# The first q and k of an attention batch, transposed at the end of the batch in front of it

## The chip, the cores and the metric

One core of one Trainium2 chip runs one program. The metric is the device time of one execution in microseconds (us). TensorE (PE) multiplies, VectorE (DVE), ScalarE (ACT) and GpSimd (POOL) work on tiles, and SyncE (SP) issues most DMAs; ACT issues some as well. Each engine goes through its own list of instructions in order, and waits where an operand or a buffer isn't ready.

## The reference

Three stages follow each other. Attention on q, k, v of 4 batches, 8 heads, 576 positions, 64 columns:

```python
q_d = q.reshape(B, H, Sd, factor, D).mean(axis=3)      # factor 4: 144 positions; k_d, v_d alike
out_d = sm_attn(q_d, k_d, v_d)
out_up = np.repeat(out_d, factor, axis=2)
mask = np.abs(pos[:, None] - pos[None, :]) < factor    # local part: 7 neighbours
scores = scale * np.matmul(q, k.transpose(0, 1, 3, 2))
...
return (out_up + out_local).astype(np.float32)
```

Its output is x, 2304 tokens of 512 columns. Then come two layers on x:

```python
h = x @ w_in                      # 512 -> 2048
g = h * (1.0 / (1.0 + np.exp(-1.702 * h)))
x = g @ w_out                     # 2048 -> 512
a = x @ w1
b = x @ w2                        # 512 -> 1024
h = a * b @ w3
return (h @ w_out).astype(np.float32)
```

## The kernel before

**Products.** Each large product is written as three matmuls of split operands (`mm3`, lines 118 to 120): low by high, high by low, high by high. The high half is a copy by ACT (line 114), the low half a subtraction, mostly by DVE (line 115).

**Stages of the program.** First `w34` is computed, the product of w3 and the second w_out (`ps_w34`, shown as `ps_w` in the trace, lines 573 to 587); its results leave through `w34s` tiles. Then the first layer goes over the tokens in blocks of 512, 512, 512, 256 and 512. In a block, `h_step` makes `ps_h` from `x_t` and w_in (4 parts kk of the 512 columns, 12 matmuls a step, 16 steps), gelu gives `g_t`, and `y_step`, two steps later, adds up `ps_y` (`ys` when it leaves). `x_t` of a block comes from `x_d` in memory: `tok_load` reads a tile `xr` on SP's queue (line 596), `tok_split` makes high and low. There are two `xr` tiles, so the read of part kk+2 waits until part kk is split. The second layer follows (`ps_ab`, `ps_o`).

**Attention.** A batch has 4 pairs of heads (HP = 4); pair n = 4b + i. A pair goes through four stages, cut into pieces: T transposes q and k (`t_piece`, line 274) and sums each group of 4 positions to `qd` and `kd`; S makes local scores (`ps_s`, line 333) and pooled scores (`ps_sp`, line 352), their maxima and exponentials `el` and `ep`; P transposes the exponentials (`ps_pt`, line 395, copied to `PT` by ACT); V multiplies with values (`ps_vp`, line 410, and `ps_v`, line 422), adds both to `xo` on DVE (line 426) and writes it to `x_d` on SP's queue (line 430). In T, batches 0 and 1 use PE transposes (`ps_t`, line 284) with ACT copies, and POOL sums (lines 294, 296); batches 2 and 3 use DVE transposes (line 280) and DVE sums (line 292).

**Loads.** `att_load` reads q and k of a pair (`s_q`, `s_k`). For the second pair of batches 1 to 3 it is called in `s_pool` (lines 343 and 344); for others in `p_piece`. A batch 0 or 1 load is issued by ACT, later ones by SP.

**What sets the order.** `att_pieces` (line 527) lists the pieces of a batch; a pump hands one out between matmuls. Batch 0 runs beside `w34`, batch b beside block b - 1, one piece for every second call. The last part kk = 3 of block 0's x needs V of pair 3, and the second block's needs V of pair 7. The pump gives only the program's order: a scheduler with costs and priorities then places each instruction on its engine, so a change in the pieces also moves work that it doesn't name. All transposes, scores and value products of attention share two PSUM tiles (tag "t"); `xo`, `w34s` and `ys` share two SBUF tiles (tag "ys").

Of the kernel before, what the change touches and what calls it, by code (L numbers as in the profile page):

```python
# [20 lines left out]
def fused_kernel(ctx, tc, q, k, v, w_in, w_out1, w1, w2, w3, w_out2, out):  # L21
    nc = tc.nc
    B, H, S, D = q.shape
# [9 lines left out]
    HP = H // 2  # L33
# [195 lines left out]
    def head_ap(src, b, hp, tok, dims):  # L229
        off = ((b * H + 2 * hp) * S + tok) * D  # L230
        return bass.AP(src.tensor, src.offset + off, dims)

    def att_load(n, names="qkv", queue=None):
        b, hp = divmod(n, HP)
        queue = queue or nc.scalar
        for name, src in (("q", q), ("k", k)):
            if name not in names:
                continue
            if b >= PE_T:

                st = att.tile([128, S // 32, 32], F32, tag="s" + name, name="s_" + name)
                for i in range(4):
                    nc.sync.dma_start(out=st[i * 32:(i + 1) * 32], in_=bass.AP(
                        src.tensor, src.offset + (b * H + 2 * hp + i // 2) * S * D + i % 2 * 32,
                        [[D, 32], [32 * D, S // 32], [1, 32]]))
                at["s" + name, n] = st
                continue
            st = att.tile([UC, 2, FAC, 2, D], F32, tag="s" + name, name="s_" + name)
            for c in range(2):
                queue.dma_start(out=st[:, c], in_=head_ap(  # L250
                    src, b, hp, c * UC * FAC, [[FAC * D, UC], [D, FAC], [S * D, 2], [1, D]]))
            at["s" + name, n] = st
        if "v" not in names:
            return
        st = att.tile([UC, 2, 2, FAC * D], F32, tag="sv", name="s_v")
        queue.dma_start(out=st, in_=head_ap(
            v, b, hp, 0, [[FAC * D, UC], [S * D, 2], [UC * FAC * D, 2], [1, FAC * D]]))
        at["sv", n] = st
# [15 lines left out]
    def t_piece(n, name, c):  # L274
        if c == 0:
            at[name, n] = att.tile([128, SD, FAC], F32, tag=name + "T", name=name + "T")
        st, dst = at["s" + name, n], at[name, n]
        if n // HP >= PE_T:
            if c == 0:
                nc.vector.transpose(dst.rearrange("p u r -> p (u r)"), st.rearrange("p a b -> p (a b)"))  # L280
        else:
            ps = pst.tile([128, FAC, UC], F32, tag="t", name="ps_t")
            for r in range(FAC):
                nc.tensor.transpose(ps[:, r], st[:, c, r].rearrange("p h d -> p (h d)"), ident[:UC, :UC])
            nc.scalar.activation(dst[:, c * UC:(c + 1) * UC].rearrange("p u r -> p r u"), ps, AF.Copy)
        if c == 1:
            if name == "q":
                d = qd[:, :SD]
            else:
                d = at["kd", n] = att.tile([128, SD], F32, tag="kd", name="kd")  # L290
            if n // HP in QK_V:
                nc.vector.tensor_reduce(d, dst, op=ALU.add, axis=X)
            else:
                nc.gpsimd.tensor_tensor(d, dst[:, :, 0], dst[:, :, 1], op=ALU.add)
                for r in range(2, FAC):
                    nc.gpsimd.tensor_tensor(d, d, dst[:, :, r], op=ALU.add)

    def v_means(n):
        sv = at.pop(("sv", n))
        nc.gpsimd.tensor_tensor(  # L300
            sv[:, :, :, :2 * D], sv[:, :, :, :2 * D], sv[:, :, :, 2 * D:], op=ALU.add)
        vd = at["vd", n] = att.tile([UC, 2, 2, D], F32, tag="vd", name="vd")
        nc.gpsimd.tensor_tensor(vd, sv[:, :, :, :D], sv[:, :, :, D:2 * D], op=ALU.add)
        if n + 1 < B * HP:
            att_load(n + 1, "v")

    def s_exp(n, i0, i1, src, scale):

        mx, sm = at["mx", n], at["sm", n]
        nb = at["nb", n][:, i0:i1]  # L310
        nc.vector.tensor_scalar(nb, mx[:, i0:i1], -scale, None, op0=ALU.mult)
        for i in range(i0, i1):
            nc.scalar.activation(
                at["el", n][:, i] if i < NQB else at["ep", n][:, i - NQB], src(i), AF.Exp, bias=nb[:, i - i0:i - i0 + 1], scale=scale,
                accum_out=sm[:, i:i + 1])

    def s_tiles(n, own_exp):
        at["ep", n] = att.tile([128, NPB, SD], F32, tag="ep", name="ep")
        for name in ("mx", "sm", "nb")[:3 if own_exp else 2]:
            at[name, n] = att.tile([128, NQB + NPB], F32, tag=name, name=name)  # L320
# [18 lines left out]
            s_exp(n, i0, i1, lambda i: e[:, i], SCALE)  # L339

    def s_pool(n, own_exp):
        if n % HP == 0 and n > 0:
            att_load(n + 1, "qk")
        near = n not in LOCAL
        if not near:
            s_tiles(n, own_exp)
        kd, ep = at["kd", n], at["ep", n]
        ps = pst.tile([128, NPB, SD], F32, tag="t", name="ps_sp")
        for j in range(NPB):
            for h in range(2):  # L350
                p = slice(h * D, (h + 1) * D)
                nc.tensor.matmul(ps[p, j], qd[p, j * PB:j * PB + QB], kd[p], start=True, stop=True)
        mx, sm = at["mx", n][:, NQB:], at["sm", n][:, NQB:]
        nc.vector.tensor_reduce(mx, ps, op=ALU.max, axis=X)
        if own_exp:
            s_exp(n, NQB, NQB + NPB, lambda i: ps[:, i - NQB], PSCALE)
        else:
            nc.vector.tensor_tensor(
                ep, ps, mx.unsqueeze(2).to_broadcast([128, NPB, SD]), op=ALU.subtract)
            if near:  # L360
                el, mxl = at["el", n], at["mx", n][:, :NQB]
                nc.vector.tensor_tensor(
                    el, el, mxl.unsqueeze(2).to_broadcast([128, NQB, KW]), op=ALU.subtract)
            nc.scalar.activation(ep, ep, AF.Exp, scale=PSCALE)
            if near:
                nc.scalar.activation(el, el, AF.Exp, scale=SCALE)
            nc.vector.tensor_reduce(sm, ep, op=ALU.add, axis=X)
            if near:
                nc.vector.tensor_reduce(at["sm", n][:, :NQB], el, op=ALU.add, axis=X)
        r = at["sm", n] if near else sm  # L370
        nc.vector.tensor_scalar_add(r, r, 1e-9)
        nc.vector.reciprocal(r, r)
        if near:
            el = at["el", n]
            (nc.vector if n // HP in NM_V else nc.gpsimd).tensor_tensor(
                el, el, r[:, :NQB].unsqueeze(2).to_broadcast([128, NQB, KW]), op=ALU.mult)
        (nc.vector if n // HP in NM_V else nc.gpsimd).tensor_tensor(
            ep, ep, sm.unsqueeze(2).to_broadcast([128, NPB, SD]), op=ALU.mult)
# [133 lines left out]
    def stage(n, what, own_exp):  # L512
        if what == "T":
            return [lambda name=name, c=c: t_piece(n, name, c) for name in "qk" for c in range(2)]
        if n in LOCAL and what in "SPV":
            if what == "S":
                return [lambda: s_pool(n, False)]
            if what == "P":
                return [lambda: p_piece(n, NPH, NPH + 4), lambda: p_piece(n, NPH + 4, NPT)]
            return [lambda: v_pool(n), lambda: l_out(n, 0, HQ), lambda: l_out(n, HQ, NQB)]  # L520
        if what == "S":
            return [lambda: s_local(n, 0, HQ, own_exp), lambda: s_local(n, HQ, NQB, own_exp), lambda: s_pool(n, own_exp)]
        if what == "P":
            return [lambda i=i: p_piece(n, i, min(i + 4, NPT)) for i in range(0, NPT, 4)]
        return [lambda: v_pool(n), lambda: v_local(n, 0, HQ), lambda: v_local(n, HQ, NQB)]

    def att_pieces(b, own_exp, rest):

        n0, out_ = b * HP, []
        for i in range(HP):  # L530
            if i == 0:
                out_ += stage(n0, "T", own_exp) + [None] * rest
            out_ += stage(n0 + i, "S", own_exp)
            if i > 0:
                out_ += stage(n0 + i - 1, "V", own_exp)
            if i + 1 < HP:
                out_ += stage(n0 + i + 1, "T", own_exp)
            else:
                out_ += [None] * rest
            out_ += stage(n0 + i, "P", own_exp)  # L540
        out_ += [None] + stage(n0 + HP - 1, "V", own_exp)
        return out_

    class Pump:
# [441 lines left out]
```

## Time and profile before

| what | value |
|---|---|
| device time, median of 3 runs | 893.88 us (893.79 to 894.19) |
| device time of the profiled execution | 894.5 us |
| its span, first to last instruction | 892.7 us |
| mean granted TensorE clock, share of full speed | 0.988 |
| PE busy | 846.7 us, 95% of the span |
| PE weight loads busy (beside matmuls) | 711.7 us, 80% |
| DVE busy | 602.2 us, 67% |
| ACT busy | 388.0 us, 43% |
| POOL busy | 146.0 us, 16% |

The profiled execution is one run under the profiler; its span is 1.8 us shorter than its device time. Times within the trace count from the start of the span. The `w34` part ends at about 122 us, block 0 at about 261 us; attention is finished before 600 us. The shares are means over stages with different limits, so a stage has to be read by itself.

### The profile page before, as it was taken

Reading aid. Unit: us, or ns where it says so; the run is one execution under the profiler, and the core shown is the slowest. Engines: PE = TensorE matmul, PEld = TensorE weight load, DVE = VectorE, ACT = ScalarE, POOL = GpSimd, SP = SyncE. Lnnn points to the kernel's source line nnn. Section 1 sums busy time; section 2 is a strip of 40 time slices with the busy share of each in tenths; the row PEclk is TensorE's granted clock in tenths of the full one; section 3 lists DMA queues with packets and bytes.
Section 4 is the critical chain, followed back from the end, with each engine's and each line's share of the span. In section 5 each row is a group of like instructions: output and inputs, shape, how many; then the busy total and the mean of one; then the engine's idle time right before and its main releaser. Section 6 shows DMA issues by size and latency. Waiting matters only on the chain.

```text
span 892.7 us, 13582 instructions
## 1 busy us (share of the span) xinstructions
PE 846.7 (95%) x5132; PEld 711.7 (80%) x5132; DVE 602.2 (67%) x1061; ACT 388.0 (43%) x750; POOL 146.0 (16%) x153
## 2 busy tenths in 40 slices
PE   5689979889999999999999999999999999999998
PEld 4567757666777777777789988889999899989996
DVE  5997597889999999747658784343556455555551
ACT  4667566567756344455336564342112211232111
POOL 7525241233232322301200000000000000000000
PEclk9799999999999999999999999999999999999999
DMA  8866574566665341543247889302556364645521
GB/s 231 271 207 164 154 234 145 155 164 179 152 188 111 78 128 43 162 98 70 64 137 277 322 305 366 130 1 68 226 186 262 107 247 165 250 140 217 196 83 71
DMA packets 140598, 150.76 MB, mean 169 GB/s; under 512 B 86898, under 2 KB 121460, under 8 KB 136436
## 3 DMA queue, kind: packets, MB, share of 16 engines
q1 hardware_dynamic: 119424, 141.21, 49.0%
q10 hardware_dynamic: 21108, 8.69, 4.3%
q8 instruction: 40, 0.66, 0.3%
q14 instruction: 26, 0.21, 0.1%
HBM read 117.75 MB, written 32.11 MB: 168 GB/s over the span
## 4 chain that ended last, share of the span: by engine, by line
PE 57%; DVE 3%; issue 1%; ACT 1%; DMA 0%; DVEq 0%; ACTq 0%
PE ps_ab L120 7%; PE ps_ab L118 7%; PE ps_ab L119 7%; PE ps_y L118 4%; PE ps_y L119 4%; PE ps_y L120 4%; PE ps_h L118 4%; PE ps_h L119 4%; PE ps_h L120 4%; PE ps_o L119 4%; PE ps_o L120 4%; PE ps_o L118 4%; DVE prod L484 1%; PE ps_pt L395 0%; DVE ql L487 0%
## 5 line engine op out<-in xcount | busy, mean ns | idle before, releaser
L118 PE MATMUL ps_h<-x_t,w 128*128 128x512 f32 (+1 forms) x320 | 122.5, 385 | 3.0 <-DVE w L115 2.6
L118 PE MATMUL ps_y<-gh,w 128*128 128x512 f32 (+1 forms) x320 | 122.0, 382 | 0.7 <-ACT gh L114 0.7
L119 PE MATMUL ps_h<-x_t,w 128*128 128x512 f32 (+1 forms) x320 | 119.0, 372 | 0.6 <-DVE x_t L115 0.6
L119 PE MATMUL ps_y<-gl,w 128*128 128x512 f32 (+1 forms) x320 | 118.5, 370 | 1.0 <-DVE gl L115 1.0
L120 PE MATMUL ps_y<-gh,w 128*128 128x512 f32 (+1 forms) x320 | 118.8, 371 | 0.0
L120 PE MATMUL ps_h<-x_t,w 128*128 128x512 f32 (+1 forms) x320 | 118.6, 371 | 0.0
L120 PE MATMUL ps_ab<-b_t,a_in 128*128 128x384 f32 x336 | 112.5, 335 | 0.0
L118 PE MATMUL ps_ab<-b_t,a_in 128*128 128x384 f32 x336 | 112.5, 335 | 0.0
L119 PE MATMUL ps_ab<-b_t,a_in 128*128 128x384 f32 x336 | 112.4, 334 | 0.0
L115 DVE TENSOR_TENSOR gl<-g_t,gh 128x512 fp32r<-128x512 f32 (+1 forms) x80 | 56.3, 706 | 55.6 <-ACT gh L114 55.1
L624 ACT ACTIVATE g_t<-ps_h 128x512 f32<-128x512 f32 (+1 forms) x80 | 44.1, 552 | 103.7 <-PE ps_h L120 102.6
L118 PEld LDWEIGHTS ps_h<-x_t,w 128*128 128x128 f32 x320 | 60.3, 189 | 17.1 <-DVE w L115 4.4
L114 ACT ACTIVATE abh<-ab 128x384 fp32r<-128x384 f32 x24 | 12.6, 526 | 137.5 <-DVE ab L749 137.5
L118 PEld LDWEIGHTS ps_y<-gh,w 128*128 128x128 f32 x320 | 60.3, 189 | 12.5 <-issue 2.2
L119 PEld LDWEIGHTS ps_h<-x_t,w 128*128 128x128 f32 x320 | 60.7, 190 | 10.5 <-DVE x_t L115 1.6
L120 PEld LDWEIGHTS ps_h<-x_t,w 128*128 128x128 f32 x320 | 60.5, 189 | 10.4 <-issue 0.2
L120 PEld LDWEIGHTS ps_y<-gh,w 128*128 128x128 f32 x320 | 60.3, 189 | 10.3
L119 PEld LDWEIGHTS ps_y<-gl,w 128*128 128x128 f32 x320 | 60.4, 189 | 10.1 <-DVE gl L115 1.3
L179 DVE SCALAR_TENSOR_TENSOR dec<-dec,st 128x512 int32<-128x512 int32 x72 | 61.3, 863 | 7.4 <-ACT dec L166 6.6
L118 PEld LDWEIGHTS ps_ab<-b_t,a_in 128*128 128x128 f32 x336 | 63.1, 188 | 0.9
L119 PEld LDWEIGHTS ps_ab<-b_t,a_in 128*128 128x128 f32 x336 | 63.1, 188 | 0.9
L120 PEld LDWEIGHTS ps_ab<-b_t,a_in 128*128 128x128 f32 x336 | 63.1, 188 | 0.0
(149 smaller groups left out, 1645.4 us busy)
## 6 DMA issues: line engine op xcount, KB each, us to landing
a_in<-a_d SPq DMA_DIRECT2D x24, 1792.0 KB
st<-in_moe_w_dram SPq DMA_DIRECT2D x32, 512.0 KB
a_d<-ap SPq DMA_DIRECT2D x8, 1792.0 KB
st<-in_moe_w_out_dram SPq DMA_DIRECT2D x24, 512.0 KB
st<-in_moe_w_in_dram SPq DMA_DIRECT2D x16, 512.0 KB
yr<-y_d SPq DMA_DIRECT2D x12, 384.0 KB
out_dram<-osb SPq DMA_DIRECT2D x17, 256.0 KB
s_v<-in_v_dram ACTq DMA_DIRECT2D x15, 288.0 KB
```

What stands on the lines that cost most here:

```text
L114: nc.scalar.activation(hi, raw, AF.Copy)
L115: lo_eng.tensor_tensor(lo, raw, f32(hi), op=ALU.subtract)
L118: nc.tensor.matmul(ps, ll, rh, start=start, stop=False, skip_group_check=more)
L119: nc.tensor.matmul(ps, lh, rl, start=False, stop=False, skip_group_check=more)
L120: nc.tensor.matmul(ps, lh, rh, start=False, stop=stop, skip_group_check=more)
L179: nc.vector.scalar_tensor_tensor(t, t, 3, st[:, :, 0], op0=ALU.logical_shift_left, op1=ALU.bitwise_or)
L484: (nc.vector if o in DVE_V else nc.gpsimd).tensor_tensor(t, at["vl", n][:, o:o + GT], s[:, o].unsqueeze(2).to_broadcast([128, GT, D]), op= ...
L624: nc.scalar.activation(g[:, :n], ps[:, :n], AF.Gelu_apprx_sigmoid)
```

## The change

`att_pieces` no longer puts T of a batch's first pair at the batch's start (except for batch 0, which has nothing in front of it). T of pair 4(b+1), four pieces, stands at the end of batch b instead, ahead of V of the batch's last pair, in place of one empty piece. The two empty pieces that followed T at the start of batches 1 to 3 go too. Batch 0 has 66 pieces where it had 63, batches 1 and 2 have 58 where they had 61, batch 3 has 39 where it had 45. The loads of q and k of the second pair of batches 1 to 3 move from `s_pool` into `t_piece`: each is issued right after the sums of the first pair's q or k.

```diff
@@ t_piece
                 for r in range(2, FAC):
                     nc.gpsimd.tensor_tensor(d, d, dst[:, :, r], op=ALU.add)
+            if n % HP == 0 and n > 0:
+                att_load(n + 1, name)
@@ s_pool
-        if n % HP == 0 and n > 0:
-            att_load(n + 1, "qk")
@@ att_pieces
-            if i == 0:
+            if i == 0 and b == 0:
                 out_ += stage(n0, "T", own_exp) + [None] * rest
...
             out_ += stage(n0 + i, "P", own_exp)
-        out_ += [None] + stage(n0 + HP - 1, "V", own_exp)
+
+        out_ += stage(n0 + HP, "T", own_exp) if b + 1 < B else [None]
+        out_ += stage(n0 + HP - 1, "V", own_exp)
```

Lines of the kernel after are two higher than before from line 297 to 342 and from line 541 on.

**First place: end of `w34`, start of block 0.** PE before, around V of pair 3 (`ps_vp` and `ps_v`; `ps_w_...` is one of the four sums of `w34`):

```order
L119 MATMUL ps_w_927<-w,w3t 128x512
L410 MATMUL ps_vp<-PT,vd 64x144 x4
L422 MATMUL ps_v<-PT,vw 64x64 x10
L120 MATMUL ps_w_927<-w,w3t 128x512
L422 MATMUL ps_v<-PT,vw 64x64 x8
L118 MATMUL ps_w_945<-w,w3t 128x512
```

Nine matmuls of `w34` and the first twelve of `ps_h` follow here before T and S of pair 4. PE after, at the same V:

```order
L120 MATMUL ps_w_980<-w,w3t 128x512
L410 MATMUL ps_vp<-PT,vd 64x144 x4
L422 MATMUL ps_v<-PT,vw 64x64 x18
L335 MATMUL ps_s<-kT,qT 64x72 x10
L118 MATMUL ps_h<-x_t,w 128x512
```

T of pair 4 now stands some twelve matmuls ahead of this V (`ps_t` from s_q, two matmuls of `w34`, `ps_t` from s_k), all of `w34` is in front of V, and the first scores of pair 4 are right behind it. SP's list before, from V's two writes to `x_d` to the read that waits for them (`w_d` is where `w34s` goes):

```order
L430 DMA x_d<-xo 128x320
L430 DMA x_d<-xo 128x256
L267 DMA vw<-in_v_dram 72x2x64
L271 DMA vw<-in_v_dram 72x4x64 x2
L271 DMA vw<-in_v_dram 72x3x64 x2
L267 DMA vw<-in_v_dram 72x2x64
L587 DMA w_d<-w34s 128x512 x2
L596 DMA xr<-x_d 128x512
```

SP's list after, the same stretch:

```order
L149 DMA st<-in_moe_w_out_dram 128x1024
L267 DMA vw<-in_v_dram 72x2x64
L271 DMA vw<-in_v_dram 72x4x64 x2
L589 DMA w_d<-w34s 128x512
L430 DMA x_d<-xo 128x320
L271 DMA vw<-in_v_dram 72x3x64 x2
L267 DMA vw<-in_v_dram 72x2x64
L142 DMA st<-in_moe_w_in_dram 128x4x256
L589 DMA w_d<-w34s 128x512
L430 DMA x_d<-xo 128x256
L149 DMA st<-in_moe_w_out_dram 128x1024
L598 DMA xr<-x_d 128x512
```

A `w34s` write now stands ahead of each `xo` write, where both `xo` writes stood first. A weight load (`st`) that came after this V's writes is ahead of them; on DVE its two decoding steps (lines 173 and 176) stand right in front of the first `xo`.

**Second place: block 0, P of pair 4.** POOL before, from the sums of pair 4 to those of pair 5:

```order
L296 TENSOR_TENSOR qd<-qd,qT 128x144 x2
L294 TENSOR_TENSOR kd<-kT 128x144
L296 TENSOR_TENSOR kd<-kd,kT 128x144 x2
L375 TENSOR_TENSOR el<-el,sm 128x648
L377 TENSOR_TENSOR ep<-ep,sm 128x432
L294 TENSOR_TENSOR qd<-qT 128x144
```

`el` scaled by its sum (line 375) is what P's transposes `ps_pt` of pair 4 read. POOL after:

```order
L302 TENSOR_TENSOR s_v<-s_v 72x4x128
L294 TENSOR_TENSOR qd<-qT 128x144
L296 TENSOR_TENSOR qd<-qd,qT 128x144 x2
L294 TENSOR_TENSOR kd<-kT 128x144
L296 TENSOR_TENSOR kd<-kd,kT 128x144 x2
L375 TENSOR_TENSOR el<-el,sm 128x648
L377 TENSOR_TENSOR ep<-ep,sm 128x432
```

The five sums shown here are those of pair 5: they stand ahead of pair 4's `el`, where they stood behind it. On PE all 16 transposes of pair 5 now stand in front of the six last matmuls of kk = 3, and pair 4's `ps_pt` right behind these.

**Third place: from block 0 to block 1.** ACT before, from the copy that makes the high half of part kk = 1 (`x_t` of line 114) to the exponential of pair 8's `el` (line 366):

```order
L114 ACTIVATE x_t<-xr 128x512
L642 ACTIVATE ys<-ps_y 128x512 x2
L473 ACT_TABLE_LOAD
L473 ACTIVATE s<-s 128x63
L114 ACTIVATE x_t<-xr 128x512 x2
L642 ACTIVATE ys<-ps_y 128x512 x2
L624 ACT_TABLE_LOAD
L624 ACTIVATE g_t<-ps_h 128x512 x2
L114 ACTIVATE gh<-g_t 128x512 x2
```

Two gelus later the exponential of `el` follows. ACT after, from the copy of part kk = 0:

```order
L114 ACTIVATE x_t<-xr 128x512
L626 ACTIVATE g_t<-ps_h 128x512
L114 ACTIVATE gh<-g_t 128x512
L473 ACT_TABLE_LOAD
L473 ACTIVATE s<-s 128x63
L644 ACTIVATE ys<-ps_y 128x512 x2
L366 ACTIVATE el<-el 128x648
L364 ACTIVATE ep<-ep 128x432
L114 ACTIVATE x_t<-xr 128x512 x2
L644 ACTIVATE ys<-ps_y 128x512 x2
L114 ACTIVATE x_t<-xr 128x512
```

Pair 8's exponentials stand ahead of the copies of parts 1 and 2, where they stood behind all four parts. On PE, after V of pair 7 there are now 36 matmuls of `ps_y` where 24 stood, then part 0 of one step (3 matmuls), `ps_s` of pair 8, part 0 of the next step (3), `ps_sp`, and then part 1; before, parts 0 and 1 of two steps (12 matmuls) stood ahead of `ps_s`.

## Rows read from the trace of the kernel before

**Rows 1.** Windows: busy us of each engine (x instructions), then granted clock, DMA share, GB/s.

```profile
122.00:137.00 15.00, 10.74 (x88) 8.35 (x87) 12.50 (x21) 8.03 (x14) 6.29 (x7) 0.89 0.85 263
255.00:270.00 15.00, 15.00 (x109) 11.65 (x105) 14.39 (x28) 9.31 (x14) 6.48 (x4) 1.00 0.75 200
```

**Rows 2.** Timeline of PE, V(3) to T(5): start, us, operation, [idle before <- releaser].

```profile
118.87 0.69 PE L422 MATMUL ps_v<-PT,vw 72*64 72x64 f32 x16
...
121.65 0.39 PE L118 MATMUL ps_h<-x_t,w 128*128 128x512 f32 x1
...
128.12 1.54 PE L333 MATMUL ps_s<-kT,qT 64*64 64x72 f32 x36
133.18 1.66 PE L352 MATMUL ps_sp<-kd,qd 64*64 64x144 f32 x12 [3.52 <-POOL kd L296]
...
136.21 0.61 PE L120 MATMUL ps_h<-x_t,w 128*128 128x512 f32 x1
...
137.12 0.41 PE L284 MATMUL ps_t<-ident,s_q 72*128 72x72 f32 x4
```

**Rows 3.** Timeline of POOL, the sums of pair 4.

```profile
130.38 0.89 POOL L294 TENSOR_TENSOR kd<-kT 128x144 f32<-128x144 f32 x1
131.35 1.77 POOL L296 TENSOR_TENSOR kd<-kd,kT 128x144 f32<-128x144 f32 x2
```

**Rows 4.** Timeline of SP's queue, a weight load and the writes of V(3).

```profile
103.43 0.38 SPq L142 DMA_DIRECT2D st<-in_moe_w_in_dram  x1
...
120.99 0.99 SPq L430 DMA_DIRECT2D x_d<-xo  x2
```

**Rows 5.** Timeline of DVE, that weight load's first decoding step, and xo of V(3).

```profile
107.55 0.43 DVE L173 TENSOR_SCALAR st<-st 128x512 int32<-128x512 int32 x1 [0.54 <-DMA st<-in_moe_w_in_dram]
...
120.49 0.48 DVE L426 TENSOR_TENSOR xo<-ps_v,od 128x320 f32<-128x320 f32 x1
```

**Rows 6.** Timeline of ACT, the wait for the write of xo, and T(4)'s copies.

```profile
124.32 1.09 ACT L586 ACTIVATE w34s<-ps_w 128x512 f32<-128x512 f32 x2 [3.07 <-DMA x_d<-xo]
...
127.37 1.39 ACT L285 ACTIVATE kT<-ps_t 128x288 f32<-128x288 f32 x2
```

**Rows 7.** Timeline of PE in block 0, where it waits in P(4).

```profile
157.36 0.63 PE L395 MATMUL ps_pt<-ident,el 128*72 128x128 f32 x4 [1.74 <-ACT kT L285]
...
161.42 0.30 PE L395 MATMUL ps_pt<-ident,el 128*72 128x128 f32 x1 [1.32 <-ACT PT L396]
```

**Rows 8.** Timeline of PE from V(7) to the first product of block 1.

```profile
254.03 1.27 PE L422 MATMUL ps_v<-PT,vw 72*64 72x64 f32 x36
...
260.84 0.39 PE L118 MATMUL ps_h<-x_t,w 128*128 128x512 f32 x1
```

**Rows 9.** Timelines of SP's queue and ACT: the read of block 1's last parts.

```profile
259.93 0.82 SPq L596 DMA_DIRECT2D xr<-x_d  x2
...
262.88 1.28 ACT L114 ACTIVATE x_t<-xr 128x512 fp32r<-128x512 f32 x2 [1.04 <-DMA xr<-x_d]
```

**Rows 10.** Groups by line: operation, count | busy us, mean ns | idle before, releasers.

```profile
L354 DVE TENSOR_REDUCE mx<-ps_sp 128x3 f32<-128x432 f32 x16 | 9.6, 599 | 9.7 <-PE ps_sp L352 9.7
L362 DVE TENSOR_TENSOR el<-el,mx 128x648 f32<-128x648 f32 x8 | 6.8, 847 | 0.0
L366 ACT ACTIVATE el<-el 128x648 f32<-128x648 f32 x8 | 5.9, 742 | 1.3 <-DVE el L362 1.2
L364 ACT ACTIVATE ep<-ep 128x432 f32<-128x432 f32 x12 | 6.7, 561 | 4.8 <-DVE ep L358 4.1 <-POOL vd L303 0.7
L280 DVE STREAM_TRANSPOSE qT<-s_q 128x576 f32<-128x576 f32 x8 | 6.1, 768 | 0.0
L367 DVE TENSOR_REDUCE sm<-ep 128x3 f32<-128x432 f32 x12 | 7.1, 594 | 2.2 <-ACT ep L364 2.2
L115 DVE TENSOR_TENSOR x_t<-xr,x_t 128x512 fp32r<-128x512 f32 (+1 forms) x20 | 13.4, 682 | 6.6 <-ACT x_t L114 6.5
L375 POOL TENSOR_TENSOR el<-el,sm 128x648 f32<-128x648 f32 x12 | 16.2, 1352 | 61.7 <-DVE sm L372 54.6 <-ACT g_t L624 4.3 <-ACT dec L166 2.9
```

## The prediction, made before the changed kernel ran

> **What bounds the kernel now.** I read the windows first. In the stretch from block 0 to block 1 PE is busy for all of its 15 us, at a granted clock of 1.00 [rows 1]; at the end of `w34` and the start of block 0 it is busy for 10.74 of 15 us, at 0.89 [rows 1]. So PE is the bound nearly everywhere, what moves to other engines is worth nothing by itself, and a change of order pays or costs only by the waits of PE that it takes away or puts in. The timeline of PE then shows the one large wait in the second stretch: after the scores of pair 4 PE stands for 3.52 us, until POOL has finished `kd` [rows 2]. POOL's rows say why: `kd` takes 0.89 and 1.77 us and starts only at 130.38 [rows 3], after the sums of q, which need T(4). T(4) itself stood late on PE. That wait is what the change is about. Behind it `ps_sp` takes 1.66 us and the products of part kk = 3 take 0.61 us where they take 0.39 us before it [rows 2]: TensorE runs at the lower of its two levels there (1.2 in place of 2.4 GHz). A mean of 0.89 over 15 us is 3.3 us at the half level, so at most 1.65 us more are lost. The old stall is worth 3.5 + 1.65 = 5.2 us. Two more waits stand in P(4), 1.74 us for ACT's copy of kT and 1.32 us for a copy to PT, 3.1 us together [rows 7]. From V(7) into block 1 there is none.
>
> **The change, part by part.** The number of products, transposes, sums and loads of q and k stays the same; they move. The work of T on PE is 16 transposes a pair, four in 0.41 us [rows 2], so 1.6 us, in the order before as after. The loads that move to `t_piece` are issued earlier or at the same place, and nothing on PE waits for them in the trace before: nothing is put down for them, and if that cover were gone it would be a wait of PE in T(5), which is inside the bounds below. Two empty pieces less at the start of a batch cost PE nothing. What counts is order, at three places.
>
> *First place, V(3) to kk = 3.* T(4) ahead of V(3) puts `kd` out of the way: the wait of 3.52 us for it goes. What is late next? V(3) itself. Before, its last products ended at 118.87 + 0.69 = 119.56, with 2.1 us of `w34` and the first products of block 0 behind it [rows 2]. Now all of `w34`, which ends at 121.65 [rows 2], and T(4), 1.6 us, stand ahead: V(3) ends near 123.3. On DVE the decoding of a weight load stands ahead of the first `xo`; such a load took 4.1 us from issue to use (103.43 to 107.55) [rows 4, 5]. How late it comes here the trace can't show; between 0 and 3 us, taken as 1.5, so the first `xo` starts near 124.9 and ends at 125.4. Its write to memory: issue at 120.99, and ACT, which waited for it, goes on at 124.32 [rows 4, 6], so 3.3 us. The second `xo` has no tile of its own until that write has landed, since a `w34s` tile now lies between the two: 125.5 + 3.3 = 128.8. With 0.5 us on DVE [rows 5] and a second write of 3.3 us it has landed at 132.6. The read of `xr` follows on SP: 2.95 us from issue to ACT's copy (259.93 to 262.88) [rows 9], 135.6. High half 0.6, low half 0.7 [rows 9, 10], then the last four products, 1.0 to 1.7 us: 138.3. Before, the same work (kk = 3, and all of T(5), which now stands ahead of it) would be over at 137.12 + 1.6 = 138.7 [rows 2]. So the old stall of 5.2 us is gone and a chain of two writes and a read, one behind the other, eats it up: -0.4 us, between -5.2 (all of the chain covered) and +2.
>
> How long a write takes decides this, so I weigh a rule on it. The rows show 3.3 us for a write and 2.95 us for a read. The Trainium skill (DMA: Bandwidth & Descriptors, Anatomy of one DMA — SWDGE (gpsimd) path) gives a DMA about 2.0 us plus its bytes at 436 GB/s, for the gpsimd path, where these are SP's. By that an estimate for 164 KB, 131 KB and 262 KB in a row is 7.3 us where the rows give 9.6, and the sum would end 2.3 us lower, at 897.8. The rows are SP's own DMAs, so I keep them.
>
> *Second place, P(4).* PE's next work behind kk = 3 is the transposes of pair 4's `el`. Before, POOL scaled `el` ahead of pair 5's sums; now these stand in front. They need T(5)'s copies of kT, and ACT makes those behind the high half of kk = 3 (136.2): the exponential of ep 0.56, kT 0.7, the exponential of el 0.74, kT 0.7 [rows 6, 10] is 138.9. Then `kd` 0.89 + 1.77 [rows 3] and `el` 1.35 [rows 10]: 142.9. PE stands from 138.3: +4.6 us. Queued behind that wait are all products of block 0's third step; who waits for them is ACT with its gelus. This gap hangs on kk = 3 with the same distance whenever that comes, so its lower end is 2 (some of POOL's sums done earlier), its upper 6. In return T(5) is long finished when P(4) runs on, and the old 3.1 us in P(4) should go; I take 2.5 of them, between 0 and 3.1.
>
> *Third place, block 0 to block 1.* Count from the end of V(7), t. Before, 24 products fill the time from 255.3 to 260.84 [rows 8], 0.23 us each; part 0 and part 1 follow, then scores. Now: 36 products 8.3, part 0 of a step 0.7, `ps_s` 1.54 [rows 2], part 0 of the next step 0.7, `ps_sp` about 1.0 (1.66 at the lower clock) [rows 2], together t + 12.2. Then PE needs the high half of part 1, which ACT makes behind pair 8's exponentials, and those need the scores just made: DVE's maximum 0.60, its subtraction 0.85, exponentials 0.74 and 0.56, copy 0.6 [rows 9, 10]: t + 15.5. PE waits 3.3 us. Two products of the high half follow (t + 16.0); the low half stands on DVE behind the subtraction of ep, a transpose of 0.77 for T(8), two sums of 0.6 to 0.85 [rows 10], and needs 0.7 itself: about t + 17.1, 1.1 us more. Sum +4.4 us where before has no wait. Bounds: 3.3 if the low half is in time, 5.9 if the read of the last part (its tile is free only after part 1 is split) and the scaling of `el` on POOL add their 1.5. The read of part 1 itself isn't late: before, a read queued behind V(7)'s writes was in use 7.6 us after V(7) ended (255.3 to 262.88) [rows 8, 9].
>
> *Elsewhere* (pair 12, blocks 1 and 2) parts 0 to 3 of the next block are split ahead of the exponentials, as before: 0, plus or minus 1.5.
>
> **The sum**: -0.4 + 4.6 - 2.5 + 4.4 = +6.1 us. Against the profiled execution of 894.5 us (span 892.7) that is 900.6; the median of the runs is 0.6 lower, so 900.0 us.
>
> **The rivals.**
> *It goes the other way, faster.* One mechanism: the chain behind V(3) is covered. If the weight load is early and POOL has the sums of pair 5 done before `el` is asked for, the old stall goes whole (-5.2), the tangle in P(4) goes too (-2.5), and the third place costs its 3.3: -4.4, 889.5 us. It decides at kk = 3: its high half would have to be on ACT before 132, four us sooner than reckoned. For it: `kd` is the largest wait of this part [rows 2], and the DMAs run at 0.85 of their share there [rows 1], so a quieter queue may be faster. Against it: the order puts V(3) 3.7 us later whatever the DMAs do.
> *It comes out even.* The first place gains 2 us more than the -0.4, the wait in P(4) is 2 in place of 4.6, the rest as reckoned: -2.4 + 2 - 2.5 + 4.4 = +1.5, 895.4, within 0.2%.
> *It is worse: the clock falls too.* The row is the old stall: 3.52 us of waiting, then products at 1.2 GHz, 1.65 us lost. The new waits of 4.6 and 3.3 us are as long; with the same loss behind each the time is 900.0 + 3.3 = 903.3. The Trainium skill (TensorE: Matmul & The Clock Gate, HAM oscillation — how this bites in real kernels) has this as a rule: a wait for data long enough makes the engine start again at the lower clock. The trace agrees after 3.52 us [rows 2].
> *It doesn't do what it says*: the transposes do stand ahead of V(3) and V(7) in the order of PE, so no chance is given to it.
>
> **How the numbers follow.** Forecast 0.52, with its own range 896 to 903; clock as well, 0.16; even, 0.17; faster, 0.15. A measurement of this kernel tells about 0.2% (1.8 us) from no change, so faster means under 892.1, slower over 895.7: 0.15, 0.17, 0.68. The predicted time is that of the likeliest case, 900.0. For the range, the upper end takes the worse case with 1.7 of the third place's and the second's upper bounds, 905; the lower end leaves out the faster case: 892.
>
> **What would show it.** In the profile after: no wait of `ps_sp` for `kd` near 130; instead a wait of `ps_s` or `ps_h` for `xo` and for the last `x_t`, two writes of `xo` over 3 us apart; a wait of `ps_pt` for `el` of line 375, 4 to 5 us, near 140; waits of `ps_h` for ACT's and DVE's `x_t` near 270, 3.3 and 1.1 us, in a stretch that had none; P(4) without its two waits. I am wrong if `x_t` of block 1 is there when PE comes to it, or if PE has other work between V(3) and kk = 3 than the list says; then the time falls under 896.

## The result: slower, and by twice what was reckoned

The changed kernel takes 906.11 us (median of 4 runs, 902.95 to 909.59); the kernel before took 893.84 in the same comparison. The ratio is 1.0145, with a 95% interval of 1.0106 to 1.0184. The direction is as forecast, the size is not: 12 us for a forecast of 6, and above the range of 892 to 905. The profiled execution took 904.0 us, 9.5 more than the one of before; times below are read from it.

PE's busy time rose from 846.7 to 851.1 us with the same 5132 instructions, and the mean granted clock fell from 0.988 to 0.975. From the page of the kernel after (engine: busy us, share of the span, instructions):

```profile
span 901.9 us, 13590 instructions
...
PE 851.1 (94%) x5132; PEld 715.5 (79%) x5132; DVE 605.7 (67%) x1061; ACT 381.3 (42%) x746; POOL 148.8 (16%) x153
```

**Where the time went.** Equal work has to be compared, so I cut both traces at the first product of a block. Block 1 starts at 260.84 before and at 260.86 after: all that happened at the end of `w34` and in block 0 comes to nothing. Block 2 starts at 379.32 and at 390.75. Block 1 alone, windows of before and of after (columns as in [rows 1]):

```profile
260.84:379.32 118.48, 117.43 (x813) 90.17 (x812) 106.21 (x174) 56.76 (x86) 36.11 (x27) 1.00 0.46 113
```

```profile
260.86:390.75 129.89, 120.88 (x813) 92.35 (x812) 104.20 (x170) 52.15 (x84) 35.95 (x26) 0.96 0.41 101
```

Both hold 813 matmuls. Block 1 is 11.4 us longer: PE is idle 9.0 us (129.89 - 120.88) in place of 1.05 (118.48 - 117.43), and busy 3.45 us longer for the same work, at a granted clock of 0.96 in place of 1.00. What follows block 1 is 2.2 us shorter (511.1 for 513.4 us to the end of the span); that goes with pair 12's move, as shown below. So the whole loss is in block 1, and about two thirds of it at its start; the rest stands between 345 and 361, where PE waits twice and the lower clock level comes back (before, the waits there are 0.50 and 0.55 us). PE after:

```profile
349.44 0.95 PE L352 MATMUL ps_sp<-kd,qd 64*64 64x144 f32 x12 [1.58 <-DVE el L338]
...
355.86 0.80 PE L422 MATMUL ps_v<-PT,vw 72*64 72x64 f32 x20 [1.64 <-issue]
...
357.01 0.63 PE L119 MATMUL ps_h<-x_t,w 128*128 128x512 f32 x1
```

**The start of block 1**, timeline of PE after. In the kernel before, block 1 starts at 260.84 [rows 8] and PE has no listed wait until 345.

```profile
260.86 0.39 PE L118 MATMUL ps_h<-x_t,w 128*128 128x512 f32 x1
...
261.63 1.35 PE L335 MATMUL ps_s<-kT,qT 64*64 64x72 f32 x36
...
266.18 0.95 PE L352 MATMUL ps_sp<-kd,qd 64*64 64x144 f32 x12 [2.31 <-DVE el L338]
270.35 1.22 PE L118 MATMUL ps_h<-x_t,w 128*128 128x512 f32 x2 [3.21 <-ACT x_t L114]
271.62 0.80 PE L119 MATMUL ps_h<-x_t,w 128*128 128x512 f32 x1
...
273.50 0.63 PE L120 MATMUL ps_h<-x_t,w 128*128 128x512 f32 x1
...
275.07 0.39 PE L119 MATMUL ps_h<-x_t,w 128*128 128x512 f32 x1
```

PE waits 2.31 us for DVE (line 338, which reads the scores of `ps_s` that came before; `ps_sp` needs their place in PSUM), then 3.21 us for the copy of part 1. The products behind take 0.63 us in place of 0.39: the lower of the two clock levels, until about 275.

**Why the copy is late.** In the timeline of ACT after, part 1 is copied behind pair 8's exponentials, at 269.68:

```profile
252.64 0.63 ACT L114 ACTIVATE x_t<-xr 128x512 fp32r<-128x512 f32 x1 [4.21 <-POOL vd L305]
...
268.58 0.74 ACT L366 ACTIVATE el<-el 128x648 f32<-128x648 f32 x1 [7.01 <-DVE el L362]
269.23 0.55 ACT L364 ACTIVATE ep<-ep 128x432 f32<-128x432 f32 x1
269.68 1.13 ACT L114 ACTIVATE x_t<-xr 128x512 fp32r<-128x512 f32 x2
```

Before, parts 0 and 1 were copied at 248.49 and 255.05, so that PE had 12 products of two steps in hand. ACT before, then PE at pair 8's first scores:

```profile
248.49 0.62 ACT L114 ACTIVATE x_t<-xr 128x512 fp32r<-128x512 f32 x1
...
255.05 0.63 ACT L114 ACTIVATE x_t<-xr 128x512 fp32r<-128x512 f32 x1 [2.22 <-POOL vd L303]
```

```profile
263.65 0.71 PE L333 MATMUL ps_s<-kT,qT 64*64 64x72 f32 x14
```

The difference starts on SP's queue. Its timeline before, around the end of block 0 (start, us of issuing):

```profile
249.24 0.38 SPq L596 DMA_DIRECT2D xr<-x_d  x1
249.66 0.97 SPq L243 DMA_DIRECT2D s_q<-in_q_dram  x2
255.84 0.34 SPq L430 DMA_DIRECT2D x_d<-xo  x1
```

And after:

```profile
245.53 1.50 SPq L243 DMA_DIRECT2D s_q<-in_q_dram  x3
247.08 2.58 SPq L243 DMA_DIRECT2D s_k<-in_k_dram  x4
254.08 1.34 SPq L430 DMA_DIRECT2D x_d<-xo  x2
...
259.14 0.85 SPq L598 DMA_DIRECT2D xr<-x_d  x2
```

The read of part 1 stood ahead of V(7)'s writes, at 249.24. After, the loads of pair 9's q and k, which the change moved into T of pair 8, stand there (eight DMAs, one of them at 242.54), and part 1 is read behind V(7)'s writes, at 259.14. SP issues nothing from 249.66 to 254.08, so it isn't the time that the loads take on the queue that makes the read late, but its place in SP's list, which is fixed when the program is built. It is in memory in good time all the same: in split_pool, below, a read issued at 260.11 is in use at 262.98, and here ACT idles for 7.01 us before the exponentials; but in ACT's list the copy now stands behind them.

**The first two places.** Timeline of PE after, from V(3) on:

```profile
117.97 1.29 PE L422 MATMUL ps_v<-PT,vw 72*64 72x64 f32 x36
122.35 1.47 PE L335 MATMUL ps_s<-kT,qT 64*64 64x72 f32 x20 [3.09 <-DVE xo L426]
...
126.47 0.63 PE L118 MATMUL ps_h<-x_t,w 128*128 128x512 f32 x1
...
136.43 0.74 PE L284 MATMUL ps_t<-ident,s_k 72*128 72x72 f32 x4 [1.32 <-DVE ep L358]
...
139.22 0.63 PE L120 MATMUL ps_h<-x_t,w 128*128 128x512 f32 x1
143.31 1.07 PE L395 MATMUL ps_pt<-ident,el 128*72 128x128 f32 x4 [3.47 <-POOL el L375]
...
147.60 0.63 PE L120 MATMUL ps_h<-x_t,w 128*128 128x512 f32 x1
...
148.99 0.40 PE L118 MATMUL ps_y<-gh,w 128*128 128x512 f32 x1
```

The first product of `ps_y` starts at 148.99; before it started at 140.37, with twelve of pair 5's transposes and four of pair 4's `ps_pt`, 1.9 us by the lengths before [rows 2], [rows 7], still to come that now stand in front. So block 0 is some 6.7 us late there, and none of it is left at 260.86.

### The profile page after: what moved, and what is told of

The parts are those of the page before. It is cut to its first block, busy times and chain, and to the rows that moved or that the text cites. A ratio compares the mean times of both kernels' runs of the same rounds, so it can differ in the third digit from the quotient of the medians.

```text
span 901.9 us, 13590 instructions
## 1 busy us (share of the span) xinstructions
PE 851.1 (94%) x5132; PEld 715.5 (79%) x5132; DVE 605.7 (67%) x1061; ACT 381.3 (42%) x746; POOL 148.8 (16%) x153
## 4 chain that ended last, share of the span: by engine, by line
PE 61%; DVE 19%; DMA 10%; issue 4%; ACT 3%; SPq 1%; POOL 1%; ACTq 0%; POOLq 0%; DVEq 0%
PE ps_ab L120 6%; PE ps_ab L118 6%; PE ps_ab L119 6%; PE ps_h L118 4%; PE ps_h L119 4%; PE ps_h L120 4%; PE ps_y L118 4%; PE ps_y L119 4%; PE ps_y L120 4%; PE ps_o L120 4%; PE ps_o L119 4%; PE ps_o L118 4%; DVE dec L179 3%; DMA st<-in_moe_w_in_dram 3%; DMA st<-in_moe_w_dram 2%
## 5 line engine op out<-in xcount | busy, mean ns | idle before, releaser
L118 PE MATMUL ps_h<-x_t,w 128*128 128x512 f32 (+1 forms) x320 | 126.4, 397 | 3.9 <-ACT x_t L114 3.7
L119 PE MATMUL ps_h<-x_t,w 128*128 128x512 f32 (+1 forms) x320 | 122.1, 382 | 0.3 <-DVE x_t L115 0.2
L120 PE MATMUL ps_h<-x_t,w 128*128 128x512 f32 (+1 forms) x320 | 121.4, 380 | 0.0
L115 DVE TENSOR_TENSOR gl<-g_t,gh 128x512 fp32r<-128x512 f32 (+1 forms) x80 | 58.5, 734 | 61.5 <-ACT gh L114 60.9
L118 PEld LDWEIGHTS ps_h<-x_t,w 128*128 128x128 f32 x320 | 62.0, 195 | 17.6 <-ACT x_t L114 4.4
L120 PEld LDWEIGHTS ps_h<-x_t,w 128*128 128x128 f32 x320 | 62.3, 195 | 11.1 <-issue 0.2
L119 PEld LDWEIGHTS ps_h<-x_t,w 128*128 128x128 f32 x320 | 62.3, 195 | 10.9 <-DVE x_t L115 2.1
L179 DVE SCALAR_TENSOR_TENSOR dec<-dec,st 128x512 int32<-128x512 int32 x72 | 57.3, 807 | 5.1 <-ACT dec L166 4.6
```

The costliest lines, as they stand in the source:

```text
L115: lo_eng.tensor_tensor(lo, raw, f32(hi), op=ALU.subtract)
L118: nc.tensor.matmul(ps, ll, rh, start=start, stop=False, skip_group_check=more)
L119: nc.tensor.matmul(ps, lh, rl, start=False, stop=False, skip_group_check=more)
L120: nc.tensor.matmul(ps, lh, rh, start=False, stop=stop, skip_group_check=more)
L179: nc.vector.scalar_tensor_tensor(t, t, 3, st[:, :, 0], op0=ALU.logical_shift_left, op1=ALU.bitwise_or)
```

## Experiments

The runs of the kernel before that stood beside these lay between 887 and 902 us, so what is compared are ratios to the runs beside them, with their intervals. "Block 1" is the time from the first product of block 1 to that of block 2 in the profiled execution, as above (118.5 before, 129.9 after). Idle is the sum of PE's listed waits in it.

| kernel | median us | ratio to before, 95% interval | block 1 starts | block 1, us | its idle, clock |
|---|---|---|---|---|---|
| before | 893.84 | 1 | 260.8 | 118.5 | 1.1, 1.00 |
| after | 906.11 | 1.0145 [1.0106, 1.0184] | 260.9 | 129.9 | 8.9, 0.96 |
| loads_only | 892.28 | 0.9995 [0.9971, 1.0020] | 258.7 | 118.4 | 1.0, 1.00 |
| t4_only | 899.42 | 1.0068 [1.0045, 1.0091] | 261.1 | 121.6 | 3.7, 1.00 |
| t4_noload | 899.09 | 1.0073 [1.0043, 1.0103] | 261.2 | 121.8 | 3.6, 1.00 |
| t4_t12 | 898.30 | 1.0049 [1.0023, 1.0074] | 261.7 | 122.9 | 3.6, 0.99 |
| t8_only | 904.21 | 1.0122 [1.0091, 1.0152] | 262.1 | 130.5 | 10.9, 0.96 |
| t8_noload | 891.65 | 0.9969 [0.9942, 0.9996] | 260.9 | 119.3 | 1.6, 1.00 |
| t8t12_noload | 890.77 | 0.9964 [0.9937, 0.9991] | 261.5 | 119.2 | 1.6, 1.00 |
| q8_only | 902.67 | 1.0060 [1.0021, 1.0099] | 255.6 | 128.4 | 7.5, 0.97 |
| after_l9 | 897.05 | 1.0049 [1.0021, 1.0078] | 263.9 | 122.7 | 5.3, 1.00 |
| t4t8_noload | 909.34 | 1.0180 [1.0122, 1.0239] | 264.1 | 129.8 | 6.9, 0.96 |
| t_noload | 903.51 | 1.0097 [1.0063, 1.0130] | 264.1 | 129.6 | 6.9, 0.96 |
| after_xo | 905.94 | 1.0144 [1.0098, 1.0190] | 259.3 | 132.3 | 11.2, 0.95 |
| split_pool | 903.22 | 1.0105 [1.0052, 1.0157] | 261.6 | 128.3 | 6.5, 0.96 |
| pad2 | 904.72 | 1.0121 [1.0057, 1.0184] | 261.2 | 128.7 | 9.3, 0.96 |
| pe_b0 | 897.96 | 1.0045 [1.0020, 1.0070] | 262.4 | 125.5 | 4.8, 0.97 |
| pe_b1 | 901.40 | 1.0089 [1.0060, 1.0118] | 260.4 | 129.2 | 3.4, 1.00 |

### Which part of the change: t4_only, t8_only, loads_only

Theory A put the loss at the start of block 1, with T of pair 8; rival B into block 0, with T of pair 4 and the lower clock.

```diff
@@ t4_only, against after
-            if i == 0 and b == 0:
+            if i == 0 and b != 1:
...
-        out_ += stage(n0 + HP, "T", own_exp) if b + 1 < B else [None]
+        out_ += stage(n0 + HP, "T", own_exp) if b == 0 else [None]
@@ t8_only, against after
-            if i == 0 and b == 0:
+            if i == 0 and b != 2:
...
-        out_ += stage(n0 + HP, "T", own_exp) if b + 1 < B else [None]
+        out_ += stage(n0 + HP, "T", own_exp) if b == 1 else [None]
```

In both, only the moved pair's load moves with it.

> Only T of pair 4 moves to the end of batch 0 (with the load of pair 5's q and k); pairs 8 and 12 as before. Theory A (the loss sits where block 0 turns into block 1, and comes with T of pair 8): within 2 us of before, 892 to 896, and no wait of PE near 260 to 275. Rival B (the loss is the chain behind V of pair 3 and the slow clock behind its waits, never given back): 900 or more.

> Only T of pair 8 moves to the end of batch 1; pairs 4 and 12 as before. Theory A: slower than before by about 8 us, 901 to 904, with ps_sp waiting some 2 us, ps_h waiting some 3 us for ACT's x_t and about ten products at the lower clock behind it. Rival B: within 3 us of before.

> The kernel before, with only the loads of pairs 5, 9 and 13 moved from the scores to the transposes. Both theories: no change that can be measured, 892 to 896. If it is over 898, the loads crowd the DMA queues and carry a part of the loss.

T of pair 8 alone loses 11 us, nearly all of the change's loss, in block 1 (130.5 us). The form differs: PE has pair 8's next transposes in its list ahead of part 1, and waits there for POOL:

```profile
275.38 1.50 PE L397 MATMUL ps_pt<-ident,el 128*72 128x128 f32 x6 [9.38 <-POOL el L377]
```

The loads by themselves cost nothing, as long as T stands where it stood. T of pair 4 fits neither theory: it loses about 6 us by the medians, but in the profiled execution (897.8 us, one of its fastest) nothing before block 1 starts (261.1); block 1 is 3.1 us longer there, and the other 3 us aren't located. So the chain behind V(3) isn't the loss, and T of pair 4 isn't free.

### Does block 0 give back what it loses: after_xo, pe_b0, pe_b1

In after_xo the chain behind V(3) is shortened; its first product of `ps_y` starts at 145.1 in place of 149.0.

```diff
@@ after_xo, against after: v_local
-        xo = g2p.tile([128, NB], F32, tag="ys", name="xo")[:, :(i1 - i0) * QB]
+        xo = g2p.tile([128, NB], F32, tag="g" if n == HP - 1 and i0 else "ys", name="xo")[:, :(i1 - i0) * QB]
@@ pe_b0 (j == 0) and pe_b1 (j == 1), against before: h_step
+            for _ in range(2 if j == 0 and 2 <= f < 8 and kk == 0 else 0):
+                mm3(ps[:, :n], w[:, 0, c], w[:, 1, c], xh[kk][:, :n], xl[kk][:, :n], True, True)
```

> The kernel after, but the second xo of pair 3 takes a tile that lies idle then (that of g_t), so it doesn't wait for the first one's write. Theory A: the last part of block 0's x comes some 3 us sooner, but the time hardly falls, 903 to 907, since block 0 gives that loss back anyway. Rival B: 3 us or more faster than the kernel after, 900 to 903.

> The kernel before with 36 products more in block 0: in six of its steps the products of part 0 are made three times, and only the last time counts. That is 36 x 0.23 = 8.2 us more of PE. If block 0's length is set by DVE, which decodes and splits weights there, most of it vanishes: 893 to 897. If PE sets it: 900 to 903.

> The kernel before with the same 36 extra products (8.2 us of PE), now in block 1: six of its steps make the products of part 0 three times, only the last counts. If block 1 is bound by PE they cost in full: 900 to 903. If it has room as block 0 had: 896 or less.

Of the 3.9 us that after_xo gains early, 1.5 are left when block 1 starts, and the time is that of the kernel after. With 8.2 us more of PE's work in block 0, block 1 starts 1.6 us later than before: block 0 has some 6.6 us of room for PE. DVE is busy there for 46.16 of 48 us in the kernel after, 47.48 before (windows 210 to 258); that DVE sets block 0's length is likely by this, but not shown. The total of pe_b0 is still 0.45% above before: in its profiled execution (902.21 us, the slowest of its runs) block 1, whose start is ordered otherwise again, is 7 us longer. With the same work in block 1 (pe_b1), that block is 10.7 us longer and the time 0.9% (8 us) more. So a us of PE's work cost little in block 0 and all of itself in block 1.

### Is it the queueing behind pair 8's exponentials: split_pool, pad2

```diff
@@ split_pool, against after: tok_split
+        if j == 1 and kk in (1, 2):
+            nc.gpsimd.tensor_copy(xh[kk][:, :n], t[:, :n])
+            nc.gpsimd.tensor_tensor(xl[kk][:, :n], t[:, :n], f32(xh[kk])[:, :n], op=ALU.subtract)
+        else:
+            split(t[:, :n], xh[kk][:, :n], xl[kk][:, :n], nc.vector)
-        split(t[:, :n], xh[kk][:, :n], xl[kk][:, :n], nc.vector)
@@ pad2, against after: att_pieces
+            if i == 0 and b == 2:
+                out_ += [None] * (4 + rest)
```

> The kernel after, but the high and low halves of parts 1 and 2 of block 1's x are made by POOL, whose list has room there, so they no longer stand behind pair 8's exponentials on ACT and its sums on DVE. Theory A (that queueing is the loss at the start of block 1): PE's wait of 3.2 us for ACT's x_t goes, the wait of ps_sp before it stays; 3 to 5 us faster than the kernel after, 900 to 903. Rival C (it only moves to the next wait): same as the kernel after, 904 to 908.

> The kernel after, with six empty pieces at the start of batch 2, as many as T and the two empty ones took before, so that pair 8's scores come as late in the program as before though T is done. On ACT parts 1 and 2 of block 1's x then stand ahead of pair 8's exponentials. Theory A: 5 to 8 us faster than the kernel after, 898 to 901. Rival D (T of pair 8 at the end of batch 1 costs by itself, where V of pair 7 comes later): 903 or more.

Both remove the wait they aim at, and the next one in the list takes its place. In split_pool the wait for `x_t` is gone, and pair 8's transposes wait, with the lower clock ahead of them and behind them; in pad2 the high half is in time, and the low half, on DVE behind pair 8's scores, isn't. PE of split_pool, then of pad2:

```profile
266.54 0.95 PE L352 MATMUL ps_sp<-kd,qd 64*64 64x144 f32 x12 [1.89 <-DVE el L338]
...
270.65 0.63 PE L120 MATMUL ps_h<-x_t,w 128*128 128x512 f32 x1
...
275.46 2.18 PE L395 MATMUL ps_pt<-ident,el 128*72 128x128 f32 x9 [3.43 <-POOL el L375]
```

```profile
267.23 1.04 PE L352 MATMUL ps_sp<-kd,qd 64*64 64x144 f32 x12 [3.18 <-DVE el L338]
...
272.69 0.79 PE L119 MATMUL ps_h<-x_t,w 128*128 128x512 f32 x1 [3.27 <-DVE x_t L115]
```

Theory A had 900 to 903 for split_pool and 898 to 901 for pad2, so it was too narrow: the queueing isn't the whole loss. What both still have in common with the kernel after is that PE comes to pair 8's scores with only part 0 of block 1 in hand.

### Why only part 0: t8_noload, after_l9, q8_only

Theory E: the moved load of pair 9 puts the read of part 1 late. In t8_noload and t_noload the edit is the kernel t8_only or after with `att_load` left in `s_pool`; in after_l9 only pair 9's is put back; q8_only moves only the first two pieces of T of pair 8.

```diff
@@ after_l9, against after
-            if n % HP == 0 and n > 0:
+            if n in (HP, 3 * HP):
                 att_load(n + 1, name)
@@ s_pool
+        if n == 2 * HP:
+            att_load(n + 1, "qk")
```

> Only T of pair 8 moves and no load does. Theory E: 892 to 897, where the same kernel with its load moved took 904. Theory A: 902 or more.

> The kernel after, with only the load of pair 9's q and k back in the scores. Theory E (that load on SP's queue ahead of part 1 is the loss): 5 us or more faster than the kernel after, 895 to 901. Theory F (with T of pair 4 moved too, block 0 ends in another order, and the start of block 1 stalls whatever that load does): 902 to 907.

> Only q's half of T of pair 8 moves, with the load of pair 9's q; k's half and its load stay at the start of batch 2. The read of part 1 stands behind V of pair 7 in this order too, and PE meets pair 8's scores ahead of part 1. Theory E and A alike: slower than before by 3 to 10 us, 896 to 903, less than with all of T.

Without the load, T of pair 8 moves for nothing or a little less than nothing (0.9969), where with it 1.0122 was measured: 1.5% hangs on where eight DMAs stand in SP's list. Part 1 is then read ahead of V(7)'s writes again, and copied ahead of the exponentials. t8_noload, SP, then ACT:

```profile
248.29 0.38 SPq L598 DMA_DIRECT2D xr<-x_d  x1
...
256.23 1.78 SPq L430 DMA_DIRECT2D x_d<-xo  x2
```

```profile
254.50 0.62 ACT L114 ACTIVATE x_t<-xr 128x512 fp32r<-128x512 f32 x1
...
263.06 1.39 ACT L114 ACTIVATE x_t<-xr 128x512 fp32r<-128x512 f32 x2
...
269.17 0.75 ACT L366 ACTIVATE el<-el 128x648 f32<-128x648 f32 x1
```

In the changed kernel itself, putting pair 9's load back (after_l9) makes block 1 7.2 us shorter (129.9 to 122.7), and the ratio falls from 1.0145 to 1.0049. That block starts 3.1 us later, though, so that at its end 4.1 of the 11.4 us are given back. What is left in it, 4.2 us, is as much as T of pairs 4 and 12 costs there without T of pair 8 (t4_t12: 122.9). In q8_only, with a half of T and of the load moved, block 1 is nearly as long as in the kernel after (128.4), but it starts 5.2 us sooner than before, so that its end is 4.7 us late.

Over all kernels, in the six whose SP reads part 1 behind V(7)'s writes (after, after_xo, split_pool, pad2, t8_only, q8_only) block 1 takes 128.3 to 132.3 us. Of the ten others without extra products it takes 118.4 to 122.9 in eight, and 129.6 and 129.8 in t_noload and t4t8_noload. So the late read comes with the loss every time, but the loss comes without it too.

### What pairs 4 and 12 cost: t4_t12, t4_noload, t4t8_noload, t8t12_noload, t_noload

> T of pairs 4 and 12 moves, T of pair 8 stays at the start of batch 2. Theory A: as with pair 4 alone, 896 to 901, so pair 12's move costs nothing. Otherwise 903 or more.

> Only T of pair 4 moves, no load. Theory F: as with its load, 897 to 902, the loss in block 1 (its length over 121 us where before has 118.5), not in block 0. Theory E: 892 to 896.

> The kernel after, but the loads of q and k of pairs 5, 9 and 13 stay in the scores, as before; only the transposes move. Theory E (the moved loads of pair 9 stand on SP's queue ahead of the read of part 1 of block 1's x; without them part 1 is read ahead of V of pair 7, as before, and PE has products of two parts in hand): 893 to 898, no wait over 1 us between 255 and 280. Theory A (pair 8's scores come too early whatever the loads do): 902 or more.

> T of pairs 4 and 8 moves, no load. Theory F: as with pair 12 too, 900 to 906. If 892 to 897, pair 12's move is what costs when no load moves.

> T of pairs 8 and 12 moves, no load; pair 4 as before. Theory F: as with pair 8 alone and no load, 889 to 894. If pair 12's move costs: 896 or more.

Pair 12's move costs nothing: t8t12_noload against t8_noload and t4_t12 against t4_only are the same within their intervals, and t_noload against t4t8_noload is 0.8% faster with it. What follows block 1 takes 509.3 to 512.2 us in the eight kernels that move it (mean 510.6) and 510.3 to 513.5 in the ten that don't (512.7), so it seems to gain some 2 us there. Pair 4's costs about 0.7% with its load or without; what of it the profiled executions show, 3.1 and 3.3 us, is in block 1. Pairs 4 and 8 together without loads lose as much in block 1 as the changed kernel, though part 1 is read early there. Theory E had 893 to 898 for t_noload, which took 903.51, so the load isn't the whole cause; t4t8_noload, at 909.34, lies above theory F's 900 to 906. PE's waits in t4t8_noload are other ones again:

```profile
267.53 0.50 PE L118 MATMUL ps_h<-x_t,w 128*128 128x512 f32 x1 [1.11 <-ACT x_t L114]
...
354.26 0.95 PE L352 MATMUL ps_sp<-kd,qd 64*64 64x144 f32 x12 [3.05 <-DVE el L336]
```

V(7)'s last products end on PE at 254.97 there, but DVE adds the second half of them only at 262.03, behind other products and sums of its own (lines 463 and 465), so the write, and the read of the part that needs it, come late. Theory F, that T of pair 4 makes block 0 end in another order and the start of block 1 stalls, isn't shown: the waits at the start, from 267 to 270, are 2.0 of that kernel's 6.9 us, and the longest stands at 354.26. Which of the moved instructions does it wasn't isolated, and after_l9, with the loads of pairs 5 and 13 moved and pair 9's not, does better than the kernel with none moved (t_noload). Why pair 4's move costs stays open.

t8t12_noload, the change without T of pair 4 and without the loads, is the fastest of all: 0.9964, with an interval that ends at 0.9991, some 3 us under the kernel before. t8_noload (0.9969) can't be told from it.

## Why the prediction went wrong, step by step

- **The loads, put down as nothing: this step failed.** The prediction says that nothing on PE waits for the moved loads, and nothing is put down for them; it looked for who waits for them, not for who stands behind them. Pair 9's eight DMAs stand on SP's queue where the read of part 1 stood, part 1 falls behind V(7)'s writes, and PE comes to pair 8's scores with part 0 alone. The working even had that read behind V(7)'s writes, but asked only whether it would be in memory in time (it was), not what had put it there, and took the third place's waits for an effect of the transposes. Measured: T of pair 8 alone has 1.0122 with that load and 0.9969 without; in the changed kernel, with that one load put back, block 1 is 7.2 us shorter and the ratio falls by 0.0096, some 8.6 us. This isn't a share that adds up with the rest: with all three loads put back (t_noload) block 1 is as long as in the changed kernel, by other waits, whose cause stays open.
- **The third place: right in place and kind, too small.** Reckoned: 3.3 us for the high half and 1.1 for the low half, 4.4 together, 5.9 as the bound. Measured: 3.21 for the high half, as worked out, and none for the low half, since the two products ahead of it took 1.22 us at the lower clock level; but also 2.31 for `ps_sp`, which the sum took as running on. It waits for DVE's `el` of line 338, and DVE had four operations of lines 484 and 487 first, 261.65 to 265.6. Later in block 1 come the two waits of 1.58 and 1.64 us. Idle time in block 1 rose by 8.0 us.
- **The lower clock, made a rival with a chance of 0.16: it came.** It made 3.45 us in block 1 alone, for the same 813 matmuls; 3.3 was the figure for both places. More than half of that is behind the start and the rest behind the wait of 1.64 us at 355.86, where none was looked for. In block 0 it came too (0.63 us a product from 123.75 to 128, from 136.9 to 139.7 and from 144 to 148.5), but block 0 gave that back.
- **The first place: the last part in time by luck, the net wrong way round.** The wait for `kd` went. V(3) ended at 119.26, not 123.3, since the work ahead of it ran sooner (PE busy for all of 90 to 106 at clock 1.00, where before had 15.37 us at 0.89). The writes and the read took 3.5, 4.3 and 4.4 us (122.32 to 125.83, 126.40 to 130.74, 130.74 to 135.16), 12.3 in all, more than the 3.3, 3.3 and 2.95 of the rows. By the Trainium skill (DMA: Bandwidth & Descriptors, Anatomy of one DMA — SWDGE (gpsimd) path) the estimate for the three was 7.3, for another path than SP's; the trace doesn't agree, and the rows are nearer to it. That SP's read waited for the second write alone isn't shown; a weight load stood in between. So the high half was on ACT at 135.16, for 135.6 in the working, because two errors of about 3 us cancelled. The last products of kk = 3 ended at 139.85, for 138.3, since they ran at the lower clock: 1.2 us later than the 138.7 of before, where 0.4 sooner was reckoned.
- **The second place: right.** 3.47 us for `el`, 4.6 reckoned (2 to 6); and in P(4) the two old waits [rows 7] are gone: PE is busy for 20.00 of the 20 us from 145 to 165.
- **What came of both: 0, not +1.7.** The working took off 2.5 us, for the two old waits in P(4); block 0 gave back all of its loss. I had read from [rows 1] that PE is the bound nearly everywhere. It isn't in block 0, where pe_b0 shows room for 6.6 us, so neither the old stall nor the new ones there had to be worth their length.
- **Elsewhere: right for pair 12**, which costs nothing: what follows block 1 is 2.2 us shorter, just past the 1.5 allowed. T of pair 4 has its cost, as far as it was located, in block 1, where none was looked for.
- **The rivals.** The faster one failed by its own point: the high half of kk = 3 was at 135.16, not before 132. The one with the clock (903.3) came nearest.

The sum with the measured sizes is 0 for block 0, 11.4 for block 1 (8.0 of waiting, 3.45 of clock) and -2.2 behind it: 9.2 us between the two profiled spans, which were 892.7 and 901.9. The medians lie 12.3 us apart; the profiled execution of the kernel after was 2.1 us under its median, and those 3 us aren't located.

## What to carry to other kernels

When a step is moved, list the DMAs it issues and look at what stands behind them on that queue: a load that is early for its own reader can push another read past a write that it then has to follow, even where the queue has time to spare. Find out for each stage whether the engine that waits is its bound, by adding work to it (as in pe_b0 and pe_b1), before a wait there is given a price; and when two stages meet, give the engine products in hand from the next stage, since with one part in hand two runs that removed a wait only uncovered the next. A wait of about 2 us also has to be given a chance of slower products behind it, which in the kernel after cost 2.3 us at the start of block 1 and 1.7 near 357 (half of the time at the lower level, an estimate from the windows).

## What the runs showed of the hardware that was not expected

Behind PE's waits of 3.1 to 3.5 us (at 122.35, 143.31 and 270.35 of the kernel after) products ran at the lower clock level for 4.5 to 6 us: 0.63 us in place of 0.39. Shorter waits brought it down as well, but not always. In split_pool, behind a wait of 1.89 us, the granted clock was 1.00 from 266.5 to 267.5 and 0.50 from 268 to 271. Behind the same product's wait at the start of block 1 it fell in t4_t12 (2.23 us; 0.63 from 274 to 277) and didn't in t4_only (2.25 us; 1.00 from 270 to 279), nor did it behind 2.10 us in after_l9 (1.00 from 279 to 288). In the kernel after it was down before the wait of 3.21 us had ended (0.50 from 268.5 to 270.3), the wait of 2.31 us having stood shortly before. A row of short waits did it too: from 131.92 to 136.91 PE had four groups of small transposes with 0.78, 1.04 and 1.32 us between them, and the products behind took 0.63 us until 139.7. So in these runs the length of the single wait doesn't tell whether the clock falls.
